# Turning attention weights in 32x32 blocks on VectorE, multiplying with v in eight 32x64 tiles, normalising on ScalarE, and rounding weights by integers

## Chip, cores, metric

One Trainium2 chip, one core. The metric is device time of one execution in microseconds; a kernel's time is the median of its runs. The kernel before: 1921.4 us (1919.91 to 1922.44, 3 runs); with the runs made beside the changed kernel 1921.06 us.

## The reference, cut to what matters

```python
# q, k, v: (8 batches, 8 heads, 576, 64) fp32, tau = 0.02
scores = (q @ k.T) / sqrt(64)
thresh = max(scores, -1) - tau
attn = exp(where(scores >= thresh, scores, -1e9) - max)
attn = attn / (sum(attn) + 1e-9);  o = attn @ v
x = o.transpose(0, 2, 1, 3).reshape(4608, 512)
out = ((x @ w_a) * (x @ w_b)) @ w_out    # w_a, w_b: 512 x 1536, w_out: 1536 x 512, float64 in memory
```

## The kernel before

Attention goes over 32 pairs of heads, five units a pair (four of 128 queries for both heads, one tail of 64 queries each). The feed-forward part of finished blocks (18 blocks of 256 rows) is woven between the units in TensorE's program, so that TensorE has work while the others prepare weights. The weights come as float64 and are turned into fp32 in 36 pieces during the first 18 units. Line numbers in the profiles (L262 and so on) are those of the kernel profiled.

```python
def weigh(i, u):                      # one unit: exp, threshold and sum, normalise
    ...
    nc.scalar.activation(w, s, AF.Exp, bias=..., scale=...)
    nc.vector.scalar_tensor_tensor(out=ws[j], in0=s, scalar=thr, in1=ws[j],
                                   op0=ALU.is_ge, op1=ALU.mult, accum_out=sums)
    nc.vector.reciprocal(rcp[:, 0:n], sums[:, 0:n])
    nc.gpsimd.tensor_scalar(w, w, rcp[:, j:j + 1], None, op0=ALU.mult)      # L262
def turn_pe(i, u):                    # keys to the partitions, by TensorE
    for s in range(4):
        nc.tensor.transpose(tp[:, s, :], w[:, c:c + P], ident)              # L287
    nc.scalar.copy(view[:, 5 * j:5 * j + 4], tp.rearrange(...))             # L288
    ...
def weighted(i, h):                   # half of a pair's queries times v: 128 keys at a time
    nc.tensor.matmul(pv, vd, wT[:, 4, :], start=True, stop=False)           # L355
    for s in range(4):
        for j in range(2):
            nc.tensor.matmul(pv[j*D:(j+1)*D], vm[:, j, s, :], wT[:, 5*j+s, :], ...)  # L358
# main loop, cut
for g in range(len(units) + PV_LAG):
    scores(i, u); turn(*before); weigh(i, u)
    for _ in range(2): convert_weights(); load_weights(1)
    advance(rate)                     # feed-forward matmuls (L388, L404)
    for what in due(g): weighted(*what)
    advance(rate)
```

Of the kernel before, what the change touches and what calls it, by code (L numbers as in the profile page):

```python
# [21 lines left out]
DMA_FROM = 32  # L22
PV_LAG = 1
WT_BUFS = 3
XT_BUFS = 4
W_BUFS = 4
# [3 lines left out]
def kernel(  # L30
# [46 lines left out]
    NSLOT = 9  # L77
    GT = HALF // TAIL
    SCALE = 1.0 / math.sqrt(D)
# [17 lines left out]
    NVD = 3  # L97
    v_diag = [const.tile([P, 2, D], FP32, name=f"v_diag{i}") for i in range(NVD)]

    def load_pair(i):  # L100
# [10 lines left out]
        vm = loads.tile([P, 2, NT, D], FP32, tag="vm", bufs=3, name="vm")  # L111
        vd = v_diag[i % NVD]
        for j in range(2):
            rows = v[b, 2 * hp + j]
            k0 = TAIL * j
            nc.sync.dma_start(vm[:, j], rows[k0:k0 + MAIN].rearrange("(s p) d -> p s d", p=P))
            k0 = MAIN * (1 - j)
            nc.sync.dma_start(vd[TAIL * j:TAIL * (j + 1), j, :], rows[k0:k0 + TAIL])
        tiles["v"] = (vm, vd)
# [23 lines left out]
    def convert_weights():  # L143
# [7 lines left out]

        if not raws:
            return
# [3 lines left out]
        t = work.tile([P, CW], FP32, tag="osb", bufs=4, name="t")  # L157
        low = work.tile([P, CW], FP32, tag="osb", bufs=4, name="low")
        top_u, t_u = top.bitcast(U32), t.bitcast(U32)
        nc.scalar.activation(low, lo, AF.Copy, bias=0.0, scale=2.0 ** -52)  # L160
        nc.vector.tensor_scalar(top_u, hi, 0x7FFFFFFF, None, op0=ALU.bitwise_and)
        nc.gpsimd.tensor_scalar(top, top, float_of(0x47F00000), float_of(0x38000000),  # L162
                                op0=ALU.min, op1=ALU.max)
        nc.vector.tensor_scalar(t_u, top_u, 3, 0x3FFFFFFF,
                                op0=ALU.logical_shift_left, op1=ALU.bitwise_and)
        nc.vector.scalar_tensor_tensor(out=top_u, in0=top_u, scalar=0x40000000, in1=t_u,
                                       op0=ALU.bitwise_and, op1=ALU.bitwise_or)
        nc.vector.tensor_scalar(t_u, top_u, 0x7F800000, None, op0=ALU.bitwise_and)
        nc.gpsimd.tensor_tensor(low, low, t, op=ALU.mult)  # L169
        nc.gpsimd.tensor_tensor(low, low, top, op=ALU.add)  # L170
        nc.vector.scalar_tensor_tensor(out=dst.bitcast(U32), in0=hi, scalar=0x80000000,
                                       in1=low.bitcast(U32),
                                       op0=ALU.bitwise_and, op1=ALU.bitwise_or)


    for t in v_diag:
        nc.gpsimd.memset(t, 0.0)
# [4 lines left out]
    ident = const.tile([P, P], FP32, name="ident")  # L182
    make_identity(nc, ident)
# [20 lines left out]
    prepared, scored, weights, turned, tbufs = {}, {}, {}, {}, {}  # L204
# [16 lines left out]
    def scores(i, u):  # L221
        qT, kT, qd = prepared[i]
        n = 2 if u < NT else 1
        sc = [ps_sc.tile([P, S], FP32, tag="sc", name="sc") for _ in range(n)]
# [19 lines left out]
    def weigh(i, u):  # L244
# [15 lines left out]
        nc.vector.reciprocal(rcp[:, 0:n], sums[:, 0:n])  # L260
        for j, w in enumerate(ws):
            nc.gpsimd.tensor_scalar(w, w, rcp[:, j:j + 1], None, op0=ALU.mult)  # L262
        weights[i, u] = ws

    def turned_tile(i, u):

        h = u // 2
        if (i, h) not in turned:
            if u < NT:
                turned[i, h] = work.tile([P, NSLOT, HALF], FP32, tag="wT", bufs=WT_BUFS, name="wT")  # L270
            else:
                turned[i, h] = work.tile([P, NSLOT, TAIL], FP32, tag="wTt", bufs=2, name="wTt")
        return turned[i, h]

    def turn_pe(i, u):

        ws = weights.pop((i, u))
        wT = turned_tile(i, u)
        if u < NT:
            view = wT.rearrange("p s (i t e) -> p s i t e", i=4, e=Q)[:, :, :, u % 2, :]  # L280
            tp = ps_1.tile([P, 4, P], FP32, tag="ps1", name="tp")
            for j, w in enumerate(ws):
                if j == 1:
                    tp = ps_1.tile([P, 4, P], FP32, tag="ps1", name="tp")
                for s in range(4):
                    c = TAIL * j + s * P
                    nc.tensor.transpose(tp[:, s, :], w[:, c:c + P], ident)  # L287
                nc.scalar.copy(view[:, 5 * j:5 * j + 4], tp.rearrange("p s (i e) -> p s i e", e=Q))  # L288
            tp = ps_1.tile([P, P], FP32, tag="ps1", name="tp")
            for j, w in enumerate(ws):  # L290
                r = slice(TAIL * j, TAIL * (j + 1))
                c = MAIN * (1 - j)
                nc.tensor.matmul(tp[r], w[:, c:c + TAIL], ident, start=True, stop=True)  # L293
            nc.scalar.copy(view[:, 4], tp.rearrange("p (i e) -> p i e", e=Q))  # L294
        else:
            w = ws[0]
            tps = []
            for j in range(2):
                r = slice(TAIL * j, TAIL * (j + 1))
                tp = ps_1.tile([P, 4, TAIL], FP32, tag="ps1", name="tp")  # L300
                for s in range(4):
                    c = TAIL * j + s * P
                    nc.tensor.transpose(tp[:, s, :], w[r, c:c + P], ident[r, r])
                tps.append(tp)
# [5 lines left out]
            for j in range(2):  # L310
                nc.scalar.copy(wT[:, 5 * j:5 * j + 4], tps[j])
                r = slice(TAIL * j, TAIL * (j + 1))
                nc.scalar.copy(wT[r, 4], tp[r, r])

    def turn_dma(i, u):


        ws = weights.pop((i, u))
        wT = turned_tile(i, u)
# [194 lines left out]
```

## Time and profile before

| | busy us | share |
|---|---|---|
| TensorE matmuls (9120) | 1799.5 | 94% |
| GpSimd | 808.2 | 42% |
| VectorE | 711.5 | 37% |
| ScalarE | 559.0 | 29% |

TensorE is dense from 336 us on; before that GpSimd is the busiest and TensorE waits. The prediction below shows the lines. One more line of that page becomes important afterwards, the fetch of TensorE's own instructions in the table of DMA queues (queue, kind: packets, MB, share of 16 engines):

```profile
q8 instruction: 72, 1.18, 0.2%
```

A fetch is 1.18 MB / 72 = 16 KB. TensorE runs 9120 matmuls and as many weight loads, 18240 / 72 = 253 instructions per fetch. Over the dense stretch such a fetch comes about every 24 us. TensorE does not wait for one there: from 336 to 1720 us its waits add up to 0.9 us, for GpSimd.

### The profile page before, as it was taken

The numbers are of one execution on the slowest core, as the hardware profiler recorded it, in microseconds if no ns is written. First come the engines' busy times: TensorE is split into PE (matmuls) and PEld (weight loads), VectorE is DVE, ScalarE is ACT, GpSimd is POOL, SyncE is SP. The second block draws the span as 40 slices with busy tenths as digits, with TensorE's granted clock in tenths as the row PEclk, the third lists the DMA queues (q8 is the fetch of TensorE's own instructions).
The fourth block names the chain that finished last, engine by engine and source line by source line (L and its number), as shares of the span: only waits on it lengthen the run. The fifth ranks groups of instructions, "written<-read, shape, count | busy, mean of one in ns | idle before, by whom it ended". The sixth has DMA issues, their size and how long they took to land.

```text
span 1917.2 us, 24375 instructions
## 1 busy us (share of the span) xinstructions
PE 1799.5 (94%) x9120; PEld 1219.7 (64%) x9120; DVE 711.5 (37%) x1650; ACT 559.0 (29%) x1185; POOL 808.2 (42%) x1047
## 2 busy tenths in 40 slices
PE   4665868999999999999999999999999999999999
PEld 2333545676757575757576767676757575758766
DVE  4666565343334333434333332332334333331000
ACT  2333322333333332333332222222323332331000
POOL 5788777434444344444444323323444344440000
PEclk9666789999999999999999999999999999999999
DMA  4223232111110111111111011001110100000000
GB/s 106 65 64 89 74 96 58 30 19 30 19 30 15 28 20 30 20 30 20 22 21 25 19 25 18 24 13 30 20 30 17 27 13 18 1 12 1 11 11 11
DMA packets 201157, 58.20 MB, mean 30 GB/s; under 512 B 191824, under 2 KB 191824, under 8 KB 201040
## 3 DMA queue, kind: packets, MB, share of 16 engines
q1 hardware_dynamic: 195792, 47.21, 11.6%
q10 hardware_dynamic: 5248, 9.44, 1.4%
q8 instruction: 72, 1.18, 0.2%
q14 instruction: 45, 0.37, 0.1%
HBM read 47.19 MB, written 9.44 MB: 30 GB/s over the span
## 4 chain that ended last, share of the span: by engine, by line
PE 84%; POOL 9%; DVE 4%; issue 2%; ACT 1%; SPq 0%; DMA 0%; POOLq 0%; DVEq 0%; ACTq 0%
PE pab L388 39%; PE po L404 20%; PE sc L229 7%; PE pv L358 6%; PE tp L287 6%; POOL w L262 4%; PE tp L293 2%; POOL low L170 2%; POOL low L169 2%; PE sc L232 2%; PE pv L355 1%; DVE w L255 1%; POOL bias L240 1%; POOL top L162 1%; DVE mx L239 1%
## 5 line engine op out<-in xcount | busy, mean ns | idle before, releaser
L262 POOL TENSOR_SCALAR w<-w,rcp 128x576 f32<-128x576 f32 x288 | 505.9, 1767 | 360.0 <-DVE rcp L260 354.0
L239 DVE TENSOR_REDUCE mx<-sc 128x1 f32<-128x576 f32 x288 | 207.3, 752 | 528.4 <-PE sc L229 458.2
L388 PE MATMUL pab<-xT,wb_sb 128*128 128x256 f32 x1536 | 389.8, 389 | 4.5 <-ACT wT L288 3.2
L404 PE MATMUL po<-wo_sb,h 128*128 128x512 f32 x864 | 389.5, 599 | 0.0
L388 PE MATMUL pab<-xT,wa_sb 128*128 128x256 f32 x1536 | 380.0, 387 | 7.2 <-ACT wT L294 7.2
L388 PEld LDWEIGHTS pab<-xT,wa_sb 128*128 128x128 f32 x1536 | 288.4, 191 | 66.0 <-issue 21.0
L388 PEld LDWEIGHTS pab<-xT,wb_sb 128*128 128x128 f32 x1536 | 287.6, 192 | 55.9 <-issue 10.5
L240 POOL TENSOR_SCALAR bias<-mx,e_nscale 128x1 f32<-128x1 f32 x288 | 95.2, 331 | 472.0 <-DVE mx L239 298.2
L255 DVE SCALAR_TENSOR_TENSOR w<-sc,thr,w 128x576 f32<-128x576 f32 x288 | 226.7, 815 | 142.0 <-ACT w L252 137.9
L404 PEld LDWEIGHTS po<-wo_sb,h 128*128 128x128 f32 x864 | 159.3, 190 | 184.0 <-issue 183.0
L288 ACT COPY wT<-tp 128x512 f32<-128x512 f32 x256 | 138.9, 588 | 415.6 <-PE tp L287 409.0
L252 ACT ACTIVATE w<-sc,bias,e_scale 128x576 f32<-128x576 f32 x288 | 230.3, 846 | 72.8 <-POOL bias L240 72.0
L398 DVE TENSOR_TENSOR h<-a,pab 128x256 f32<-128x256 f32 x216 | 90.6, 420 | 405.7 <-PE pab L388 405.3
L229 PE MATMUL sc<-kT,qT 64*128 64x512 f32 (+1 forms) x1024 | 200.8, 474 | 39.1 <-DVE w L255 30.9
L229 PEld LDWEIGHTS sc<-kT,qT 64*128 64x128 f32 x1024 | 105.9, 198 | 163.6 <-issue 153.3
L287 PE MATMUL tp<-ident,w 128*128 128x128 f32 x1024 | 152.5, 291 | 51.2 <-POOL w L262 51.1
L395 ACT COPY a<-pab 128x256 f32<-128x256 f32 x216 | 80.7, 374 | 364.0 <-PE pab L388 363.9
L287 PEld LDWEIGHTS tp<-ident,w 128*128 128x128 f32 x1024 | 116.9, 148 | 67.1 <-POOL w L262 61.3
L358 PE MATMUL pv<-wT,vm 128*64 128x256 f32 x1024 | 132.7, 404 | 0.0
L358 PEld LDWEIGHTS pv<-wT,vm 128*64 128x64 f32 x1024 | 71.3, 144 | 54.6 <-issue 29.2
L241 POOL TENSOR_SCALAR thr<-mx,cut 128x1 f32<-128x1 f32 x288 | 85.8, 298 | 0.0
L363 ACT COPY xT<-pv 128x256 f32<-128x256 f32 x64 | 23.8, 372 | 199.1 <-PE pv L358 186.6
(55 smaller groups left out, 990.4 us busy)
## 6 DMA issues: line engine op xcount, KB each, us to landing
qm<-in_q_dram SPq DMA_DIRECT2D x128, 72.0 KB, 2.4
km<-in_k_dram SPq DMA_DIRECT2D x128, 72.0 KB, 2.5
vm<-in_v_dram SPq DMA_DIRECT2D x64, 128.0 KB, 2.5
out_dram<-osb ACTq DMA_DIRECT2D x32, 256.0 KB, 2.0
raw<-in_moe_w_a_dram SPq DMA_DIRECT2D x12, 512.0 KB, 3.8
raw<-in_moe_w_b_dram SPq DMA_DIRECT2D x12, 512.0 KB, 3.8
raw<-in_moe_w_out_dram SPq DMA_DIRECT2D x12, 512.0 KB, 3.7
v_diag<-in_v_dram SPq DMA_DIRECT2D x64, 16.0 KB, 2.0
```

What stands on the lines that cost most here:

```text
L229: nc.tensor.matmul(sc[j][:, c0:c1], qT[r, u * P:(u + 1) * P], kT[r, c0:c1], start=True, stop=True)
L239: nc.vector.tensor_reduce(mx[:, c], sc[j], axis=AX.X, op=ALU.max)
L240: nc.gpsimd.tensor_scalar(bias[:, c], mx[:, c], e_nscale[:, 0:1], None, op0=ALU.mult)
L252: nc.scalar.activation(w, s, AF.Exp, bias=bias[:, j:j + 1], scale=e_scale[:, 0:1])
L255: nc.vector.scalar_tensor_tensor(out=ws[j], in0=s, scalar=thr[:, j:j + 1], in1=ws[j], op0=ALU.is_ge, op1=ALU.mult, accum_out=sums[:, j:j + 1])
L262: nc.gpsimd.tensor_scalar(w, w, rcp[:, j:j + 1], None, op0=ALU.mult)
L287: nc.tensor.transpose(tp[:, s, :], w[:, c:c + P], ident)
L288: nc.scalar.copy(view[:, 5 * j:5 * j + 4], tp.rearrange("p s (i e) -> p s i e", e=Q))
L358: nc.tensor.matmul(pv[j * D:(j + 1) * D], vm[:, j, s, :], wT[:, 5 * j + s, :], start=False, stop=(s == 3))
L388: nc.tensor.matmul(p, w[:, c, fs], xT[:, c, :], start=(c == 0), stop=(c == HP - 1))
L398: nc.vector.tensor_tensor(hid, a, pab[1], op=ALU.mult)
L404: nc.tensor.matmul(po, hs[F][:, u * P:(u + 1) * P], wo_sb[:, F, :], start=(F == 0), stop=(F == NF - 1))
```

## The change

The intent: take the transposes off TensorE, the bound engine. VectorE's transpose, as used here (0.77 us for 128x576 in the trace), turns each block of 32x32 in its place, which leaves the keys of each quarter of queries on a partition quadrant of their own; so v is loaded into all four quadrants, and the product is made of eight small tiles (four quadrants of 32 keys, two heads of 64 columns). ScalarE normalises instead of GpSimd, and the conversion of weights needs two buffers a piece instead of three and ends in an integer addition.

```diff
-            nc.gpsimd.tensor_scalar(w, w, rcp[:, j:j + 1], None, op0=ALU.mult)
+            nc.scalar.activation(w, w, AF.Copy, scale=rcp[:, j:j + 1])
...
+        for j in range(2):                       # instead of turn_pe
+            nc.vector.transpose(tb[r, j * NB:(j + 1) * NB, e],
+                                w[r].rearrange("p (n e) -> p n e", e=Q))
...
+        for h in range(2):                       # instead of the five matmuls a half
+            tb = turned.pop((i, h))
+            for c in range(NB):                  # 18 blocks of 32 keys
+                for g in range(G):               # 4 quadrants
+                    for j in range(2):           # 2 heads
+                        n = 3 * Q if h == 1 and g // 2 == j else 2 * Q
+                        nc.tensor.matmul(pv[g][jc, c0:c0 + n], vr[r, j * NB + c, :],
+                                         tb[r, j * NB + c, 0:n],
+                                         start=(c == 0), stop=(c == NB - 1))
...
+        for g in range(G):                       # v, four times
+            nc.sync.dma_start(vr[g * Q:(g + 1) * Q], rows)
...
-        t = work.tile([P, CW], FP32, tag="osb", bufs=4, name="t")
...
-        nc.gpsimd.tensor_tensor(low, low, t, op=ALU.mult)
-        nc.gpsimd.tensor_tensor(low, low, top, op=ALU.add)
-        nc.vector.scalar_tensor_tensor(out=dst.bitcast(U32), in0=hi, scalar=0x80000000,
-                                       in1=low.bitcast(U32),
-                                       op0=ALU.bitwise_and, op1=ALU.bitwise_or)
+        nc.gpsimd.tensor_tensor(dst.bitcast(U32), top_u, low_u, op=ALU.add)
...
-        advance(rate)
-        for what in due(g):
-            weighted(*what)
+        advance(1.7 * rate)
+        if g > NT and g % (NT + 1) == 0:
+            done = g // (NT + 1) - 1
+            weighted(done)
...
-        advance(rate)
+        advance(0.3 * rate)
```

A piece of weights now takes two buffers of the four instead of three, and three instructions on ScalarE, two on VectorE and two on GpSimd instead of one, five and three. The product of a whole pair is one run of matmuls, once every five units.

More of the change, by code (lines that the diff above doesn't have):

```diff
@@ L20, in float_of @@
     return struct.unpack("<f", struct.pack("<I", bits))[0]
-DMA_FROM = 32
-PV_LAG = 1
-WT_BUFS = 3
 XT_BUFS = 4
-W_BUFS = 4
+W_BUFS = 5
+TB0_BUFS = 2
+TB1_BUFS = 1
 @with_exitstack
@@ L76 @@
     HALF = MAIN // 2
-    NSLOT = 9
     GT = HALF // TAIL
+    G = P // Q
+    BANK = 512
     SCALE = 1.0 / math.sqrt(D)
@@ L96 @@
     loaded = {}
-    NVD = 3
-    v_diag = [const.tile([P, 2, D], FP32, name=f"v_diag{i}") for i in range(NVD)]
     def load_pair(i):
@@ L110, in load_pair @@
             tiles[name] = t
-        vm = loads.tile([P, 2, NT, D], FP32, tag="vm", bufs=3, name="vm")
-        vd = v_diag[i % NVD]
-        for j in range(2):
-            rows = v[b, 2 * hp + j]
-            k0 = TAIL * j
-            nc.sync.dma_start(vm[:, j], rows[k0:k0 + MAIN].rearrange("(s p) d -> p s d", p=P))
-            k0 = MAIN * (1 - j)
-            nc.sync.dma_start(vd[TAIL * j:TAIL * (j + 1), j, :], rows[k0:k0 + TAIL])
-        tiles["v"] = (vm, vd)
+        vr = loads.tile([P, 2 * NB, D], FP32, tag="vr", bufs=2, name="vr")
+        rows = v[b, 2 * hp:2 * hp + 2].rearrange("j (n e) d -> e (j n) d", e=Q)
+        for g in range(G):
+            nc.sync.dma_start(vr[g * Q:(g + 1) * Q], rows)
+        tiles["v"] = vr
         loaded[i] = tiles
@@ L156, in convert_weights @@
         top = work.tile([P, CW], FP32, tag="osb", bufs=4, name="top")
-        t = work.tile([P, CW], FP32, tag="osb", bufs=4, name="t")
         low = work.tile([P, CW], FP32, tag="osb", bufs=4, name="low")
-        top_u, t_u = top.bitcast(U32), t.bitcast(U32)
-        nc.scalar.activation(low, lo, AF.Copy, bias=0.0, scale=2.0 ** -52)
-        nc.vector.tensor_scalar(top_u, hi, 0x7FFFFFFF, None, op0=ALU.bitwise_and)
-        nc.gpsimd.tensor_scalar(top, top, float_of(0x47F00000), float_of(0x38000000),
+        top_u, low_u = top.bitcast(U32), low.bitcast(U32)
+        nc.scalar.activation(top, hi.bitcast(FP32), AF.Abs)
+        nc.scalar.activation(low, lo, AF.Copy, bias=2.0 ** 23, scale=2.0 ** -29)
+        nc.gpsimd.tensor_scalar(top, top, float_of(0x47EFFFFF), float_of(0x38000000),
                                 op0=ALU.min, op1=ALU.max)
-        nc.vector.tensor_scalar(t_u, top_u, 3, 0x3FFFFFFF,
+        nc.scalar.activation(low_u, low, AF.Copy, bias=-(2.0 ** 23), scale=1.0)
+        nc.vector.tensor_scalar(top_u, top_u, 3, 0x3FFFFFFF,
                                 op0=ALU.logical_shift_left, op1=ALU.bitwise_and)
-        nc.vector.scalar_tensor_tensor(out=top_u, in0=top_u, scalar=0x40000000, in1=t_u,
+        nc.vector.scalar_tensor_tensor(out=top_u, in0=hi, scalar=0xC0000000, in1=top_u,
                                        op0=ALU.bitwise_and, op1=ALU.bitwise_or)
-        nc.vector.tensor_scalar(t_u, top_u, 0x7F800000, None, op0=ALU.bitwise_and)
-        nc.gpsimd.tensor_tensor(low, low, t, op=ALU.mult)
-        nc.gpsimd.tensor_tensor(low, low, top, op=ALU.add)
-        nc.vector.scalar_tensor_tensor(out=dst.bitcast(U32), in0=hi, scalar=0x80000000,
-                                       in1=low.bitcast(U32),
-                                       op0=ALU.bitwise_and, op1=ALU.bitwise_or)
-    for t in v_diag:
-        nc.gpsimd.memset(t, 0.0)
+        nc.gpsimd.tensor_tensor(dst.bitcast(U32), top_u, low_u, op=ALU.add)
     tau_sb = const.tile([P, 1], FP32, name="tau_sb")
@@ L181 @@
     load_weights(2)
-    ident = const.tile([P, P], FP32, name="ident")
-    make_identity(nc, ident)
     q_diag = [const.tile([P, P], FP32, name=f"q_diag{i}") for i in range(2)]
@@ L201 @@
     nc.vector.tensor_tensor(cut, cut, big, op=ALU.add)
-    prepared, scored, weights, turned, tbufs = {}, {}, {}, {}, {}
+    prepared, scored, weights, turned = {}, {}, {}, {}
     x_of, xtail_of = {}, {}
@@ L223, in scores @@
         n = 2 if u < NT else 1
-        sc = [ps_sc.tile([P, S], FP32, tag="sc", name="sc") for _ in range(n)]
+        sc = [ps_sc.tile([P, 2 * BANK], FP32, tag="sc", name="sc")[:, 0:S] for _ in range(n)]
         for c0, c1 in ((0, MAIN), (MAIN, S)):
@@ L260, in weigh, with turn @@
         nc.vector.reciprocal(rcp[:, 0:n], sums[:, 0:n])
+        weights[i, u] = (ws, rcp)
+    def turn(i, u):
+        ws, rcp = weights.pop((i, u))
         for j, w in enumerate(ws):
-            nc.gpsimd.tensor_scalar(w, w, rcp[:, j:j + 1], None, op0=ALU.mult)
-        weights[i, u] = ws
-    def turned_tile(i, u):
-        h = u // 2
-        if (i, h) not in turned:
-            if u < NT:
-                turned[i, h] = work.tile([P, NSLOT, HALF], FP32, tag="wT", bufs=WT_BUFS, name="wT")
-            else:
-                turned[i, h] = work.tile([P, NSLOT, TAIL], FP32, tag="wTt", bufs=2, name="wTt")
-        return turned[i, h]
@@ L275, in turn_pe @@
-    def turn_pe(i, u):
-        ws = weights.pop((i, u))
-        wT = turned_tile(i, u)
-        if u < NT:
-            view = wT.rearrange("p s (i t e) -> p s i t e", i=4, e=Q)[:, :, :, u % 2, :]
-            tp = ps_1.tile([P, 4, P], FP32, tag="ps1", name="tp")
-            for j, w in enumerate(ws):
-                if j == 1:
-                    tp = ps_1.tile([P, 4, P], FP32, tag="ps1", name="tp")
-                for s in range(4):
-                    c = TAIL * j + s * P
-                    nc.tensor.transpose(tp[:, s, :], w[:, c:c + P], ident)
-                nc.scalar.copy(view[:, 5 * j:5 * j + 4], tp.rearrange("p s (i e) -> p s i e", e=Q))
-            tp = ps_1.tile([P, P], FP32, tag="ps1", name="tp")
-            for j, w in enumerate(ws):
-                r = slice(TAIL * j, TAIL * (j + 1))
-                c = MAIN * (1 - j)
-                nc.tensor.matmul(tp[r], w[:, c:c + TAIL], ident, start=True, stop=True)
-            nc.scalar.copy(view[:, 4], tp.rearrange("p (i e) -> p i e", e=Q))
-        else:
-            w = ws[0]
-            tps = []
-            for j in range(2):
-                r = slice(TAIL * j, TAIL * (j + 1))
-                tp = ps_1.tile([P, 4, TAIL], FP32, tag="ps1", name="tp")
-                for s in range(4):
-                    c = TAIL * j + s * P
-                    nc.tensor.transpose(tp[:, s, :], w[r, c:c + P], ident[r, r])
-                tps.append(tp)
-            tp = ps_1.tile([P, P], FP32, tag="ps1", name="tp")
-            for j in range(2):
-                r = slice(TAIL * j, TAIL * (j + 1))
-                c = MAIN * (1 - j)
-                nc.tensor.matmul(tp[r], w[:, c:c + TAIL], ident, start=True, stop=True)
-            for j in range(2):
-                nc.scalar.copy(wT[:, 5 * j:5 * j + 4], tps[j])
-                r = slice(TAIL * j, TAIL * (j + 1))
-                nc.scalar.copy(wT[r, 4], tp[r, r])
@@ L315, in turn_dma @@
-    def turn_dma(i, u):
-        ws = weights.pop((i, u))
-        wT = turned_tile(i, u)
-        if u < NT:
-            if u % 2 == 0:
-                tbufs[i] = work.tile([P, 2 * NB, 2 * Q], FP32, tag="tb", bufs=2, name="tb")
-            tb = tbufs[i]
-            for j, w in enumerate(ws):
-                nc.vector.transpose(
-                    tb[:, j * NB:(j + 1) * NB, (u % 2) * Q:(u % 2 + 1) * Q],
-                    w.rearrange("p (n e) -> p n e", e=Q))
-            if u % 2 == 0:
-                return
-            src = tb.rearrange("p (s r) e -> p s r e", r=4)
-            for g in range(4):
-                for r in range(4):
-                    nc.sync.dma_start(
-                        wT[r * Q:(r + 1) * Q, :, g * 2 * Q:(g + 1) * 2 * Q],
-                        src[g * Q:(g + 1) * Q, :, r, :])
-        else:
-            tb = work.tile([P, NB, Q], FP32, tag="tbt", bufs=2, name="tbt")
-            nc.vector.transpose(tb.rearrange("p n e -> p (n e)"), ws[0])
-            for g in range(4):
-                j = g // 2
-                for r in range(4):
-                    s = [s for s in range(NSLOT) if 0 <= 4 * s + r - j * NB < NB]
-                    b0 = 4 * s[0] + r - j * NB
-                    nc.sync.dma_start(
-                        wT[r * Q:(r + 1) * Q, s[0]:s[-1] + 1, (g % 2) * Q:(g % 2 + 1) * Q],
-                        tb[g * Q:(g + 1) * Q, b0:b0 + 4 * len(s) - 3:4, :])
@@ L348, in weighted @@
-    def weighted(i, h):
-        b, hp = pairs[i]
-        wT = turned.pop((i, h))
-        vm, vd = loaded[i]["v"]
-        n = HALF if h < 2 else TAIL
-        pv = ps_1.tile([P, n], FP32, tag="ps1", name="pv")
-        nc.tensor.matmul(pv, vd.rearrange("p j d -> p (j d)"), wT[:, 4, :], start=True, stop=False)
-        for s in range(4):
-            for j in range(2):
-                nc.tensor.matmul(pv[j * D:(j + 1) * D], vm[:, j, s, :], wT[:, 5 * j + s, :],
-                                 start=False, stop=(s == 3))
-        if h < 2:
-            if hp == 0:
-                x_of[b, h] = work.tile([P, HP, HALF], FP32, tag="xT", bufs=XT_BUFS, name="xT")
-            nc.scalar.copy(x_of[b, h][:, hp, :].rearrange("p (t i e) -> p i t e", t=2, e=Q),
-                           pv.rearrange("p (i t e) -> p i t e", t=2, e=Q))
-            if hp == HP - 1:
-                blocks.append((x_of.pop((b, h)), ("half", b, h)))
-        else:
-            t = b % GT
-            if hp == 0 and t == 0:
-                xtail_of[b // GT] = work.tile([P, HP, HALF], FP32, tag="xt", bufs=2, name="xt")
-            xt = xtail_of[b // GT]
-            nc.scalar.copy(xt[:, hp, t * TAIL:(t + 1) * TAIL], pv)
-            if hp == HP - 1 and t == GT - 1:
@@ new lines, in turn @@
+            nc.scalar.activation(w, w, AF.Copy, scale=rcp[:, j:j + 1])
+        h = min(u // 2, 1)
+        if u == 0:
+            turned[i, 0] = work.tile([P, 2 * NB, 2 * Q], FP32, tag="tb0", bufs=TB0_BUFS, name="tb0")
+        if u == 2:
+            turned[i, 1] = work.tile([P, 2 * NB, 3 * Q], FP32, tag="tb1", bufs=TB1_BUFS, name="tb1")
+        tb = turned[i, h]
+        e = slice((u - 2 * h) * Q, (u - 2 * h + 1) * Q)
+        for j in range(2):
+            r = slice(0, P) if u < NT else slice(j * D, (j + 1) * D)
+            w = ws[j] if u < NT else ws[0]
+            nc.vector.transpose(tb[r, j * NB:(j + 1) * NB, e],
+                                w[r].rearrange("p (n e) -> p n e", e=Q))
@@ new lines, in weighted @@
+    def weighted(i):
+        b, hp = pairs[i]
+        vr = loaded[i]["v"]
+        pvs = [ps_sc.tile([P, 2 * BANK], FP32, tag="sc", name="pv") for _ in range(2)]
+        pv = [pvs[g // 2][:, (g % 2) * BANK:(g % 2 + 1) * BANK] for g in range(G)]
+        c0 = 0
+        for h in range(2):
[4 more added lines that the diff above has]
+                        n = 3 * Q if h == 1 and g // 2 == j else 2 * Q
+                        r = slice(g * Q, (g + 1) * Q)
+                        jc = slice(j * D, (j + 1) * D)
+                        nc.tensor.matmul(pv[g][jc, c0:c0 + n], vr[r, j * NB + c, :],
+                                         tb[r, j * NB + c, 0:n],
+                                         start=(c == 0), stop=(c == NB - 1))
+            c0 += 2 * Q
+        t = b % GT
+        if hp == 0:
+            for h in range(2):
+                x_of[b, h] = work.tile([P, HP, HALF], FP32, tag="xT", bufs=XT_BUFS, name="xT")
+            if t == 0:
+                xtail_of[b // GT] = work.tile([P, HP, HALF], FP32, tag="xt", bufs=2, name="xt")
+        xt = xtail_of[b // GT][:, hp, t * TAIL:(t + 1) * TAIL]
+        for gg in range(2):
+            for h in range(2):
+                x = x_of[b, h][:, hp, :].rearrange("p (t g e) -> p t g e", t=2, g=G)
+                nc.scalar.copy(
+                    x[:, :, 2 * gg:2 * gg + 2, :],
+                    pvs[gg].rearrange("p (g c) -> p g c", g=2)[:, :, 2 * Q * h:2 * Q * (h + 1)]
+                    .rearrange("p g (t e) -> p t g e", t=2))
+            jc = slice(gg * D, (gg + 1) * D)
+            nc.scalar.copy(xt[jc].rearrange("p (g e) -> p g e", g=2),
+                           pvs[gg][jc].rearrange("p (g c) -> p g c", g=2)[:, :, 4 * Q:5 * Q])
+        if hp == HP - 1:
+            for h in range(2):
+                blocks.append((x_of.pop((b, h)), ("half", b, h)))
+            if t == GT - 1:
@@ L374, in weighted @@
                 blocks.append((xtail_of.pop(b // GT), ("tail", b - t, 0)))
-            del loaded[i], prepared[i]
+        del loaded[i], prepared[i]
     def ffn(xT, what):
@@ L442 @@
     UB = HP * (NT + 1)
-    def turn(i, u):
-        (turn_dma if i >= DMA_FROM else turn_pe)(i, u)
-    def due(g):
-        got = []
-        for d, first, last in ((PV_LAG, 1, 1), (PV_LAG, 3, 3), (PV_LAG, 4, 4)):
-            if g - d >= 0 and units[g - d][1] == last:
-                got.append((units[g - d][0], last // 2))
-        return got
     prep(0)
@@ L457 @@
     rate = 0.0
-    for g in range(len(units) + PV_LAG):
+    for g in range(len(units) + 2):
         if g < len(units):
             i, u = units[g]
-            if u == 0 and i + 1 < NPR:
+            if u == 1 and i + 1 < NPR:
                 load_pair(i + 1)
@@ L474 @@
             before = (i, u)
-        advance(rate)
-        for what in due(g):
-            weighted(*what)
-            if what[1] == 1 and what[0] % HP == HP - 1:
+        advance(1.7 * rate)
+        if g > NT and g % (NT + 1) == 0:
+            done = g // (NT + 1) - 1
+            weighted(done)
+            if pairs[done][1] == HP - 1:
                 rate = backlog() / (2 * UB)
-        advance(rate)
+        advance(0.3 * rate)
     advance(float("inf"))
```

## The prediction

> **What bounds the kernel now.** I read the page first: busy shares, the slices of the span, the chain of waits by engine.
>
> ```profile
> PE 1799.5 (94%) x9120; PEld 1219.7 (64%) x9120; DVE 711.5 (37%) x1650; ACT 559.0 (29%) x1185; POOL 808.2 (42%) x1047
> ...
> PE   4665868999999999999999999999999999999999
> ...
> POOL 5788777434444344444444323323444344440000
> PEclk9666789999999999999999999999999999999999
> ...
> PE 84%; POOL 9%; DVE 4%; issue 2%; ACT 1%; SPq 0%; DMA 0%; POOLq 0%; DVEq 0%; ACTq 0%
> ```
>
> There are two stages. In the first seven slices (to 336 us) TensorE is at 4 to 8 tenths, GpSimd at 7 to 8, and the granted clock is low. From 336 us to the end TensorE never stops; there only TensorE work counts. So I need TensorE's work per pair of heads and the idle time of the first stage. The work I take from the timeline of TensorE in the dense stretch, as the distance from one group's start to the next (the ends are modelled):
>
> ```profile
> 1009.57 0.59 PE L355 MATMUL pv<-wT,v_diag 128*128 128x256 f32 x2
> 1010.09 1.95 PE L358 MATMUL pv<-wT,vm 128*64 128x256 f32 x16
> 1011.97 1.99 PE L388 MATMUL pab<-xT,wa_sb 128*128 128x256 f32 x8
> ...
> 1020.21 0.33 PE L355 MATMUL pv<-wTt,v_diag 128*128 128x64 f32 x2
> 1020.47 0.69 PE L358 MATMUL pv<-wTt,vm 128*64 128x64 f32 x16
> 1021.08 1.13 PE L388 MATMUL pab<-xT,wb_sb 128*128 128x256 f32 x4
> ...
> 1024.30 1.30 PE L229 MATMUL sc<-kT,qT 64*128 64x512 f32 x8
> 1025.53 1.09 PE L287 MATMUL tp<-ident,w 128*128 128x128 f32 x8
> 1026.55 0.44 PE L293 MATMUL tp<-ident,w 128*64 128x128 f32 x4
> 1026.92 1.56 PE L388 MATMUL pab<-xT,wb_sb 128*128 128x256 f32 x6
> ```
>
> The scores of a unit take 1025.53 - 1024.30 = 1.23 us, its transposes 1.39 us; half a product with v takes 2.40 us, its tail 0.87 us. A pair has four such units and a tail unit (in the same timeline scores about 1.0, transposes 0.76). Per pair: scores 5.9, transposes 4 x 1.39 + 0.76 = 6.3, product 2 x 2.40 + 0.87 = 5.7 us. One block of the feed-forward part, undisturbed at the end, takes 41.4 + 20.6 = 62.0 us (192 and 48 matmuls in the chain of waits), 18 blocks 1117 us. In the dense stretch its matmuls take 32 us more than that rate, at the handovers. Sum: 32 x 17.9 + 1117 + 32 = 1722 us, so about 195 us of 1917 is TensorE idle or slow, nearly all in the first stage.
>
> The first stage, by stretches of the span (columns: stretch, length, busy us of PE, PEld, DVE, ACT, POOL, clock, DMA share, GB/s) and groups of instructions:
>
> ```profile
> 20.00:240.00 220.00, 146.70 (x661) 85.08 (x662) 132.83 (x276) 73.21 (x139) 173.72 (x191) 0.71 0.29 72
> ...
> L262 POOL TENSOR_SCALAR w<-w,rcp 128x576 f32<-128x576 f32 x288 | 505.9, 1767 | 360.0 <-DVE rcp L260 354.0
> ...
> L170 POOL TENSOR_TENSOR low<-low,top 128x512 f32<-128x512 f32 x36 | 47.7, 1326 | 2.3
> L169 POOL TENSOR_TENSOR low<-low,t 128x512 f32<-128x512 f32 x36 | 45.6, 1267 | 32.2 <-DVE t L168 16.3 <-DVE sums L258 8.9 <-DVE rcp L260 5.9
> ...
> L213 DVE STREAM_TRANSPOSE qT<-qm 128x576 f32<-128x576 f32 x32 | 24.6, 768 | 1.5 <-DMA qm<-in_q_dram 1.5
> ```
>
> GpSimd is busy 79% of this stretch: per unit 1.8 normalisations of 1.77 us, plus two weight pieces of 0.63 + 1.27 + 1.33 us, plus 1.1 us of small work: 10.8 us. The reciprocals show 20 units done at 218 us, 10.9 us each, and the 36th piece of weights at 328 us, 9 us apiece: a piece takes three of four buffers, so pieces go one at a time.
>
> [...] in the tail product two matmuls start 6 to 7 ns apart in every 58 ns, and each mode change leaves about 0.15 us. [...] No stretch of this trace shows a sustained rate above about 70 instructions a microsecond. [...] the trace has 72 fetches of 16 KB.
>
> **The change, part by part.**
> - *Transposes off TensorE*: -6.3 us per pair, -202 us. VectorE gets ten block transposes of 0.77 us per pair, 7.7 us (+246 us), beside TensorE: its load of 37% rises to near 50%.
> - *The product with v*: 18 key blocks x 8 tiles x 2 parts of queries = 288 fp32 products a pair, each two passes: 576 matmuls and 576 weight loads, against about 66 matmuls now. Call its time X. A pass of 64 columns lasts 58 ns (tail product); 96 columns scale to about 85. With all eight tiles at once X = 18 x 2 x (58 + 85) ns + two drains = 5.5 us. That needs a pass every 7 ns or so, weight load included, kept up over 1152 instructions. I doubt that and allow 7 ns for each instruction, weight load or matmul: X = 8.1 us.
> - *Normalising to ScalarE*: GpSimd loses 506 us; ScalarE gains 288 x about 0.7 us (from its 0.59 us for 512 columns) = 200 and loses the copies of transposes (139 + 36 + 21 + 13 = 209 us). Both are hidden when dense.
> - *Integer rounding*: a piece costs GpSimd 0.63 + 1.3, VectorE two instructions of 0.43 and 0.73 instead of five of 3.1 in all, ScalarE three of about 0.67. With two buffers of four, two pieces can be on their way.
> - *v to four quadrants*: 4608 packets of 256 bytes a pair instead of 1152, about 5 us of all DMA engines at 18.5 ns each; hidden when dense, felt in the first stage.
>
> First stage after: per unit GpSimd 5.0 us, ScalarE 1.8 x (0.85 + 0.7) + 4.0 + 0.4 = 7.2, VectorE 1.4 + 1.5 + 1.6 + 2.3 + 0.7 = 7.5. With waits between them 8.5 us: the 20 units until the feed-forward part can start take 170 us, of which TensorE works 4 x (5.9 + about 7) = 50. Idle: 120 us instead of 195. DMA needs about 135 us there (18.9 MB of weights at 200 GB/s plus 41 of q, k, v), under 170.
>
> Dense work: 1117 + 32 x 5.9 = 1306, plus 24 for fewer handovers. The product takes both score buffers of PSUM, and only 0.3 of a share of feed-forward work (about 1 us) covers its six copies out (1.5 to 2 us on ScalarE): about 0.8 us stall a pair, 25 us. End 5 us. Span = 1306 + 24 + 120 + 25 + 5 + 32 X = 1480 + 32 X. With X = 8.1: 1739 us; I say 1740.
>
> **Rivals.**
> 1. *Full packing*, X = 5.5: 1656 us. For it: two row tiles (scores) and two column tiles already overlap fully. Against it: no trace line has more than two tiles.
> 2. [...]
> 3. *Only two tiles overlap*[...]: X = 288 x 58 ns + 1.9 = 18.6, 2075 us. Against it: in the trace two passes of *different* tiles start together[...].
> 4. *Fetch of instructions*: 74 KB per burst, a 16 KB fetch takes about 1 us in the trace. If buffers hold little, X is about 9 to 15.
> 5. *Another engine becomes the bound*: VectorE near 50% and ScalarE near 35% speak against it outside the first stage.
>
> **Range and chances.** The first stage is worth 75 us in nearly any case; the rest hangs on X, with break-even at (1917 - 1480) / 32 = 13.7 us. I give full packing to 8 us 40%, 8 to 12.4 us 26%, 12.4 to 15 us (within 2% of even, or just under) 8%, above that 26%. Range 1645 to 2000; faster 0.66, same 0.08, slower 0.26.
>
> **What would show it.** TensorE's timeline should have one burst of 576 matmuls per pair: its length is X[...]. The reciprocal of the 20th unit should come near 170 us, the last weight piece before it. GpSimd should fall near 260 us busy, VectorE rise near 880. A gap after the burst, ended by ScalarE's copies, should be under 1 us. I am wrong if the burst takes over 13.7 us, if the engine waits in it for instructions, or if the first stage stays near 300 us because another chain (weights, DMA) takes GpSimd's place.

Some figures above have no line beside them; these are of the same trace. One fp32 product of the program is two matmuls in it (L355: one call a half, x2). The scores' matmuls (64 rows, 512 columns) start in twos, 7 ns apart, every 430 ns, where the feed-forward ones of 512 columns start singly every 429 ns. The 0.15 us of a mode change is the distance from the last start of the tail product (1020.93) to the next group (1021.08), and the two drains in X are two of these. The 36864 packets of 256 bytes took 18.5 ns in the mean. The 200 GB/s is an estimate from the first 20 us, 165 GB/s at a DMA share of 0.81. The 7 ns allowed for each instruction is an estimate; what was measured beside it are the starts 6 to 7 ns apart.

## The result

| | before | changed |
|---|---|---|
| time, median us (range) | 1921.06 (1919.91 to 1922.44) | 1980.62 (1978.76 to 1984.01) |
| VectorE / ScalarE / GpSimd busy us | 711.5 / 559.0 / 808.2 | 878.5 / 621.7 / 246.6 |
| TensorE matmul instructions | 9120 | 23904 |
| reciprocal of the 20th unit, us | 217.6 | 209.9 |
| last piece of weights, us | 327.9 | 245.8 |

The ratio is 1.031 (95% interval 1.029 to 1.033): slower. Ratios in this document are the mean time of one kernel's fast runs over that of the other's of the same rounds, so not quite the ratio of the medians quoted.

The page of the changed kernel: busy shares, slices, DMA queue of TensorE's instructions, the chain of waits by engine, the product's group.

```profile
PE 1717.4 (87%) x23904; PEld 1239.8 (63%) x23904; DVE 878.5 (44%) x1862; ACT 621.7 (31%) x1129; POOL 246.6 (12%) x718
...
PE   2565598889998998899989999889998998989999
...
PEclk9765598999989888899999998889989998999999
...
q8 instruction: 188, 3.08, 0.7%
...
PE 85%; issue 9%; DVE 3%; POOL 2%; ACT 1%; DMA 0%; SPq 0%; DVEq 0%; POOLq 0%
...
L282 PE MATMUL pv<-tb,vr 32*64 32x64 f32 (+1 forms) x18432 | 314.5, 282 | 170.5 <-issue 170.4
```

Before, TensorE was at nine tenths in every slice from the eighth on. Now eights and nines alternate, and the granted clock dips with them. The new thing in the chain is "issue", up from 2% to 9%: time in which the engine waited for nothing that the profile shows. TensorE's waits of this kind all stand before one line, the product with v: 170 us. The timeline of one product in the dense stretch shows where:

```profile
998.16 0.59 PE L321 MATMUL pab<-xT,wa_sb 128*128 128x256 f32 x2
998.69 3.22 PE L282 MATMUL pv<-tb,vr 32*64 32x64 f32 x274
1003.79 1.78 PE L282 MATMUL pv<-tb,vr 32*64 32x64 f32 x128 [1.88 <-issue]
1007.53 1.82 PE L282 MATMUL pv<-tb,vr 32*64 32x64 f32 x128 [1.97 <-issue]
1011.55 0.85 PE L282 MATMUL pv<-tb,vr 32*64 32x64 f32 x46 [2.20 <-issue]
1012.34 2.63 PE L321 MATMUL pab<-xT,wa_sb 128*128 128x256 f32 x6
1014.90 1.87 PE L215 MATMUL sc<-kT,qT 64*128 64x512 f32 x8
```

The 576 matmuls run in stretches with a stop of about 2 us between them, and the stretches inside are of exactly 128. With a weight load each, 128 matmuls are 256 instructions: one fetch (3.08 MB / 188 = 16 KB here too, and 47808 / 188 = 254 instructions). In all 32 products the first stop (over 0.5 us) comes after 86 to 274 matmuls, and the later ones 128 apart, but for one of the first stage.

The DMA records of the trace, counted from the start of the span like the lines above, have fetches that start at 997.92, 1001.37, 1004.90 and 1009.12 us, 3.5 to 4.2 us apart instead of 24. The last three take 0.9 to 1.3 us, and TensorE goes on 1.3 to 1.5 us after each has landed. It is so at all 111 stops of the 32 products: each ends 0.4 to 1.6 us (median 1.4) after a fetch has landed.

From 998.69 to 1012.34 the product takes 13.65 us; the mean over the 32 products is 14.9 us, of which 5.9 us are stops. Stops are counted here, and in all runs below, as distances of over 0.5 us from one matmul's start to the next, 190 us in all; the profile's idle time is a little less, 157 us inside the products and 14 us before them.

Two smaller things are in the same lines. Inside a stretch the eight tiles do run together: the first 32 matmuls of this burst start 6 to 7 ns apart in rounds of eight, the second and third round 58 to 59 ns long (the first is 106), as long as two tiles took for one pass each of 64 columns in the tail product before (58 ns). From the 33rd on the pace slackens to 11 to 12 ns a matmul in the first half of the columns. And after the burst six feed-forward matmuls take 2.56 us up to the next group where six take 1.3 elsewhere, and a score group takes 1.79 us instead of 1.23: the granted clock was halved (0.5 in the clock records). In this case the record runs from 1012.7 to 1016.1 us, where the feed-forward matmuls start 427 ns apart instead of 216. After 400 us there are 222 us of such time, against 2 us in the kernel before, which lie behind its last matmul; here each halved stretch but the one at the very end (4 us) begins inside a product or at most 0.4 us after it.

The first stage, as a stretch of the span, answers to the line the prediction shows of before:

```profile
20.00:240.00 220.00, 117.43 (x2476) 84.65 (x2477) 134.67 (x262) 116.86 (x198) 89.70 (x146) 0.67 0.54 116
```

GpSimd fell from 173.72 to 89.70 us, ScalarE rose from 73.21 to 116.86, and TensorE is busy even less than before. The times of the reciprocals show why: most units follow each other within 12 us, but after the first unit of a pair, where the product of the pair before stands in the program, there are 34, 25, 24 and 27 us. With no feed-forward work beside it the first four bursts lasted 17.0, 17.3, 15.8 and 15.9 us (after the first, TensorE waited 6.1 us more for a copy on ScalarE); the clock was halved for 9, 61, 100 and 78% of them.

### The profile page after: what moved, and what is told of

Its sections match the earlier page's. It is cut to its first block, busy times and chain, and to the rows that moved or that the text cites. A ratio compares the mean times of both kernels' runs of the same rounds, so it can differ in the third digit from the quotient of the medians.

```text
span 1976.9 us, 53536 instructions
## 1 busy us (share of the span) xinstructions
PE 1717.4 (87%) x23904; PEld 1239.8 (63%) x23904; DVE 878.5 (44%) x1862; ACT 621.7 (31%) x1129; POOL 246.6 (12%) x718
## 3 DMA queue, kind: packets, MB, share of 16 engines
q8 instruction: 188, 3.08, 0.7%
## 4 chain that ended last, share of the span: by engine, by line
PE 85%; issue 9%; DVE 3%; POOL 2%; ACT 1%; DMA 0%; SPq 0%; DVEq 0%; POOLq 0%
PE pab L321 39%; PE po L337 19%; PE pv L282 15%; PE sc L215 9%; PE sc L218 2%; DVE w L241 1%; DVE top L161 1%; DVE mx L225 1%; POOL top L156 0%; POOL wa_sb L163 0%; DVE tb L264 0%; DVE top L159 0%; POOL bias L226 0%; ACT w L253 0%; ACT w L238 0%
## 5 line engine op out<-in xcount | busy, mean ns | idle before, releaser
L282 PE MATMUL pv<-tb,vr 32*64 32x64 f32 (+1 forms) x18432 | 314.5, 282 | 170.5 <-issue 170.4
L282 PEld LDWEIGHTS pv<-tb,vr 32*64 32x64 f32 x18432 | 282.5, 163 | 208.3 <-issue 201.4
L321 PE MATMUL pab<-xT,wa_sb 128*128 128x256 f32 x1536 | 399.9, 397 | 6.1 <-ACT xT L296 6.1
L321 PE MATMUL pab<-xT,wb_sb 128*128 128x256 f32 x1536 | 374.4, 383 | 0.0
L264 DVE STREAM_TRANSPOSE tb<-w 128x576 f32<-128x576 f32 (+1 forms) x320 | 239.3, 767 | 123.8 <-ACT w L253 123.1
L253 ACT ACTIVATE w<-w,rcp 128x576 f32<-128x576 f32 x288 | 212.7, 771 | 194.0 <-DVE rcp L246 194.0
L215 PEld LDWEIGHTS sc<-kT,qT 64*128 64x128 f32 x1024 | 115.6, 211 | 199.8 <-issue 174.4
L296 ACT COPY xT<-pv 128x128 f32<-128x128 f32 x128 | 27.7, 272 | 430.0 <-PE pv L282 429.2
L341 ACT COPY osb<-po 128x512 f32<-128x512 f32 x36 | 20.8, 579 | 116.1 <-PE po L337 116.1
L218 PE MATMUL sc<-kT,q_diag 128*128 128x64 f32 (+1 forms) x128 | 42.8, 461 | 10.4 <-DVE w L241 10.4
```

Source lines behind the costliest of these rows:

```text
L215: nc.tensor.matmul(sc[j][:, c0:c1], qT[r, u * P:(u + 1) * P], kT[r, c0:c1], start=True, stop=True)
L253: nc.scalar.activation(w, w, AF.Copy, scale=rcp[:, j:j + 1])
L264: nc.vector.transpose(tb[r, j * NB:(j + 1) * NB, e], w[r].rearrange("p (n e) -> p n e", e=Q))
L282: nc.tensor.matmul(pv[g][jc, c0:c0 + n], vr[r, j * NB + c, :], tb[r, j * NB + c, 0:n], start=(c == 0), stop=(c == NB - 1))
L321: nc.tensor.matmul(p, w[:, c, fs], xT[:, c, :], start=(c == 0), stop=(c == HP - 1))
```

## The experiments

The theory after reading: TensorE runs out of instructions. The first stop came after 172 to 548 of them (86 to 274 matmuls), 256 more came with each fetch, 3.5 to 4.2 us apart in the burst shown, and the product asks for 1152 in a row. Rivals: the stops belong to the tiles (PSUM, data, array); or the cost lies in another part of the change.

| run | what | us (median) | ratio to before | 95% interval |
|---|---|---|---|---|
| changed kernel | | 1980.62 | 1.031 | 1.029 to 1.033 |
| e1_four_tiles | four tiles overlap instead of eight | 2113.23 | 1.100 | 1.099 to 1.102 |
| e2_pieces | the product in four pieces | 1851.77 | 0.965 | 0.962 to 0.967 |
| e3_one_tb | half the instructions | 1725.78 | 0.899 | 0.897 to 0.900 |
| e4_rounding_only | before + conversion | 1867.34 | 0.972 | 0.971 to 0.974 |
| e5_norm_only | before + ScalarE normalises | 1878.48 | 0.978 | 0.976 to 0.979 |
| e6_one_tb_two_pieces | e3, product in two pieces | 1702.05 | 0.886 | 0.885 to 0.888 |
| e7_one_tb_four_tiles | e3 with four tiles | 1849.53 | 0.963 | 0.962 to 0.965 |
| e8_one_tb_early_qk | e6, q and k earlier | 1701.23 | 0.886 | 0.884 to 0.887 |
| e9_rounding_and_norm | before + both | 1846.10 | 0.962 | 0.960 to 0.964 |
| e10_convert_last | e6, conversion later | 1704.53 | 0.887 | 0.886 to 0.889 |

All ten results were correct against the reference.

**e3_one_tb: the same columns in half the instructions**

```diff
-turned[i, 0]: [P, 2 * NB, 2 * Q] (2 buffers);  turned[i, 1]: [P, 2 * NB, 3 * Q] (1 buffer)
+turned[i] = work.tile([P, 2 * NB, 5 * Q], FP32, tag="tb", bufs=1, name="tb")
-        for h in range(2):
-            for c in range(NB):  ... n = 64, or 64 and 96
+        for c in range(NB):      ... n = 160, or 128
```

> The changed kernel with one buffer for all turned weights of a pair, so that one matmul takes 160 or 128 columns instead of two of 64 and 64 or 96: half the instructions for the same columns. Fetch theory: 576 instructions a burst instead of 1152[...]; 36 passes of 0.138 us = 5.0 us, drains, and at most one or two gaps: burst 6 to 8 us, time 1700 to 1760 us. Rival (columns streamed, or the array, set the burst): burst stays near 14 us, time 1960 to 1990 us.

Measured 1725.78 us, as expected; the rival is out. One product of it:

```profile
871.82 3.33 PE L276 MATMUL pv<-tb,vr 32*64 32x160 f32 x177
876.05 2.16 PE L276 MATMUL pv<-tb,vr 32*64 32x160 f32 x111 [0.90 <-issue]
878.13 1.56 PE L314 MATMUL pab<-xT,wa_sb 128*128 128x256 f32 x6
```

There is one stop where there were three or four, of 0.90 us where those were of about 2, and the burst lasts 6.3 us. Over all products the median is 6.4 us and the stops are 1.0 us a product (5.9 in the changed kernel). The halved clock after 400 us fell from 222 us to 4 us, all of it at the very end (mean granted clock 0.961 against 0.901). The columns streamed are the same.

**e2_pieces: the same instructions, spread**

```diff
+                if (h * NB + c + 1) % 9 == 0 and h * NB + c + 1 < 2 * NB:
+                    between()        # lambda: advance(0.67 * rate)
-        advance(1.7 * rate) before each product, advance(0.3 * rate) after
+        1.2 before, 0.67 in each of three pauses, 0.3 after; 1.625 in the other units
```

> The changed kernel, the same matmuls of the product cut into four pieces with about 2 us of feed-forward matmuls between them (as much feed-forward work as before over a pair). Fetch theory: nearly all the 170 us in which the product waits for issue go; against it four more changes of tiling mode a pair at about 0.2 us each (25 us in all); time 1830 to 1870 us. Rival (the waits belong to PSUM, the array or the data of the product, not to the fetch): the waits stay, time 1980 to 2010 us.

Measured 1851.77 us, as expected. Two of the four pieces of one product, and what lies around them:

```profile
934.10 1.80 PE L282 MATMUL pv<-tb,vr 32*64 32x64 f32 x144
...
939.05 1.80 PE L282 MATMUL pv<-tb,vr 32*64 32x64 f32 x144
940.78 1.13 PE L324 MATMUL pab<-xT,wa_sb 128*128 128x256 f32 x4
```

A piece of 144 matmuls runs through in 1.73 us (940.78 - 939.05), 12 ns each, with no stop inside. The waits for issue went from 170 to 78 us, not to "nearly all": 41 us of them lie after 300 us (134 in the changed kernel). The rest is in the first stage, where there is no feed-forward work to put between the pieces. The same matmuls stall or don't according to how densely they stand in the program: together with the fetches that land 0.4 to 1.6 us before each restart in the changed kernel, that is the supply of instructions, not the tiles. The halved clock after 400 us fell to 43 us (mean granted clock 0.949).

**e1_four_tiles: half the overlap**

```diff
-            for c in range(NB):
-                for g in range(G):
+            for g0 in (0, 2):
+              for c in range(NB):
+                for g in (g0, g0 + 1):
```

> The changed kernel, but the product runs over two quadrants of v first and then over the other two, so four tiles can overlap instead of eight; same instructions, same columns. Theory (the burst is paced by the fetch of instructions, 256 at a time every 3.5 us): the stretches of 128 matmuls get longer and the gaps between them shorter, the burst stays 14.5 to 15.5 us, time 1975 to 2010 us. Rival (the burst is paced by how many tiles overlap): stretches of 128 matmuls double from about 1.8 and 2.8 us, gaps stay near 2 us, burst about 21 us, time about 2180 us.

Measured 2113.23 us: a miss for both. The burst took 17.8 us in the mean (15.5 expected at most), though its stops shrank from 5.9 to 2.2 us as the theory said.

```profile
1068.43 4.11 PE L283 MATMUL pv<-tb,vr 32*64 32x64 f32 x273
1074.18 3.04 PE L283 MATMUL pv<-tb,vr 32*64 32x64 f32 x128 [1.64 <-issue]
1077.93 6.75 PE L283 MATMUL pv<-tb,vr 32*64 32x96 f32 x175 [0.70 <-issue]
1084.61 2.93 PE L322 MATMUL pab<-xT,wa_sb 128*128 128x256 f32 x6
```

The first 273 matmuls run at 15 ns, what four tiles give at the full clock (58 / 4). The last 175 take 38 ns each instead of the 21 that I estimate for 96 columns (85 / 4, with the prediction's 85), and the feed-forward matmuls after them are twice as long as usual. The clock was halved in the middle of the burst; the mean granted clock was 0.866 against 0.901, and the halved time after 400 us 420 us against 222. So a burst with half the tiles and stops costs clock as well. I had not reckoned with the clock, and this run can't separate the two.

**e7_one_tb_four_tiles: the overlap again, without the stops**

```diff
-        for c in range(NB):
-            for g in range(G):
+        for c, g in [(c, g0 + d) for g0 in (0, 2) for c in range(NB) for d in range(2)]:
```

> e3_one_tb, but two quadrants of v first, then the other two: four tiles overlap instead of eight, same instructions. With the fetch out of the way the overlap should count: 72 passes of 0.138 us = 9.9 us instead of 5.0, less the gap: burst 9.9 to 10.5 us instead of 6.4 (7.4 in the mean, with the first pairs), time 1835 to 1880 us, provided the granted clock stays at full. If the overlap of eight isn't real: no change from 1726 us.

Measured 1849.53 us, as expected: 124 us over e3.

```profile
953.52 9.54 PE L275 MATMUL pv<-tb,vr 32*64 32x160 f32 x288
962.99 1.56 PE L313 MATMUL pab<-xT,wa_sb 128*128 128x256 f32 x6
```

The burst has no stop: 288 matmuls with their weight loads in 9.47 us are 16.4 ns an instruction, and the changed kernel was supplied with 256 every 3.5 us or so, 14 ns each. A pass takes 9.47 / 72 = 0.132 us (0.138 was the estimate), and after 400 us the clock is full but for 4 us at the very end (0.956 in the mean of the run, first stage included). Eight tiles against four are worth 9.47 - 6.4 = 3.1 us a product, and 4.2 us against the 5.3 us of the next run, which has no stop either. The packing of eight tiles works; it was hidden behind the fetch in the changed kernel (5.9 us of stops a product).

**e6_one_tb_two_pieces: half the instructions and spread**

```diff
+            if (c + 1) % 9 == 0 and c + 1 < NB:
+                between()            # lambda: advance(0.5 * rate)
-        1.7 and 0.3 around the product; 2.0 in the other units
+        1.7, 0.5 and 0.4;              1.85 in the other units
```

> e3_one_tb with the product cut once in the middle, about 1.5 us of feed-forward matmuls in between. Fetch theory: the one gap of about 1 us a pair (32 us in all) goes, two mode changes of 0.1 to 0.2 us come: time 1695 to 1720 us against 1726. Rival (the gap isn't the fetch): the gap stays, 1726 to 1740 us.

Measured 1702.05 us, as expected: both pieces go in 2.66 us each without a stop, 5.3 us in all. (Before the dense stretch 12 us of waits for issue remain.)

```profile
860.56 2.73 PE L276 MATMUL pv<-tb,vr 32*64 32x160 f32 x144
863.22 0.70 PE L316 MATMUL pab<-xT,wa_sb 128*128 128x256 f32 x2
...
866.00 2.73 PE L276 MATMUL pv<-tb,vr 32*64 32x160 f32 x144
868.66 1.56 PE L316 MATMUL pab<-xT,wa_sb 128*128 128x256 f32 x6
```

**e4_rounding_only, e5_norm_only and e9_rounding_and_norm: the other parts on the kernel before**

e4 takes the two-buffer conversion with integer rounding into the kernel before, e5 this one line, e9 both:

```diff
-            nc.gpsimd.tensor_scalar(w, w, rcp[:, j:j + 1], None, op0=ALU.mult)
+            nc.scalar.activation(w, w, AF.Copy, scale=rcp[:, j:j + 1])
```

> The kernel before with only the new conversion of the weights (two buffers a piece, integer rounding). Theory of the prediction: in the first stage the pieces of weights no longer go one at a time, the last piece comes before 230 us instead of 328 us, dense work starts earlier; time 1860 to 1890 us. Rival (GpSimd's normalisations keep the first stage where it is): 1910 to 1925 us.

> The kernel before with only the normalisation moved from GpSimd to ScalarE. Theory (in the first stage the pieces of weights go one at a time and set its end; GpSimd's normalisations only share its time): the last piece comes a little sooner, before 328 but after 280 us, time 1890 to 1920 us. Rival (GpSimd's load of 79% sets the first stage): the last piece before 240 us, time about 1860 us.

> The kernel before with the new conversion of the weights and the normalisation on ScalarE, that is, the change without its third part (turning by VectorE, eight tiles, v in four quadrants). Alone they gave 53 and 42 us. Theory (both shorten the first stage only, and share what they shorten): 1825 to 1855 us, so the third part costs 125 to 155 us. Rival (the changed kernel's first stage gained all that is to be had, or one part hides the other): 1860 us or more.

Rounding alone: 1867.34 us, the last piece of weights at 214 us instead of 328, as expected. Normalisation alone: 1878.48 us, a larger gain than the theory's 1890 to 1920 us, with the last piece at 284 us. I take it that the pieces still go one at a time and GpSimd is freer between them; no run tests that. Both: 1846.10 us, the last piece at 187 us, the 20th unit at 190 us. The same stretch as above, of e9:

```profile
20.00:240.00 220.00, 176.69 (x846) 107.86 (x846) 128.06 (x264) 155.56 (x287) 98.10 (x166) 0.75 0.40 105
```

GpSimd is at 45% (79% before) and TensorE gained 30 us in this stretch. So these two parts give 75 us, and the third part (turning, tiles, v four times) costs 1980.6 - 1846.1 = 134.5 us on top of them.

**e8_one_tb_early_qk and e10_convert_last: the first stage of e6**

```diff
 e8
-            if u == 1 and i + 1 < NPR: load_pair(i + 1)
+            if u == 0 and i + 1 < NPR: load_pair(i + 1)     # q, k
+            if u == 1 and i + 1 < NPR: load_v(i + 1)
 e10
-            convert_weights(); load_weights(1)  (twice)  before the product
+            the same at the end of the unit, after it
```

> e6 with q and k of the next pair asked for one unit earlier than v (as early as the kernel before did). Theory (three waits for q and k in the first stage, 32 us in e3, come from the later loads and from v's four-fold loads ahead in the queue): the waits go, time 20 to 35 us under e6. Rival (they are only replaced by other waits of the first stage): within 10 us of e6.

> e6 with the conversion of weights asked for at the end of a unit, behind the product and its copies, instead of before them. Theory (after the first pair TensorE waits 20.7 us because ScalarE, which now has three conversion steps a piece, does conversions ahead of the copy of the product that the next matmul needs): that wait goes, time 1670 to 1695 us against 1702. Rival (the conversions are needed anyway and another wait takes its place): 1695 to 1710 us.

In both the theory missed and the rival came true: 1701.23 and 1704.53 us, within 3 us of e6. In e8 the waits for k fell from 31.8 to 16.2 us, and those for the product's copies on ScalarE rose from 22.7 to 36.2 us. In e10 the longest wait for the first copy,

```profile
PE pab L316 <- ACT xT L291: 20.7, 1, 20.7
```

(this is e6: TensorE's waits, columns total, times, longest) fell to 15.3 us only, and other waits grew. The first stage has several chains of nearly the same length; what sets its end with the small product stays open.

## Why the prediction was wrong

The direction was wrong: 1740 us and a gain of 9% foretold, 1980.6 us and a loss of 3% measured, though inside the wide range. The sum "1480 + 32 X" was nearly right: with the measured X of 14.9 us it gives 1957 us of span, and the span was 1976.9. That is partly luck: the 25 us allowed for copies measured 7, which hides part of what the first stage and the clock cost more. Two of the prediction's own signs of being wrong came true: the burst took over 13.7 us, and the engine waited in it for instructions.

- **The step that failed** is "I doubt that and allow 7 ns for each instruction, weight load or matmul: X = 8.1 us." The matmuls outside the stops did take that: 14.9 - 5.9 = 9.0 us with the stretches at a halved clock in it. What the term left out are the stops, 5.9 us a product, 190 us in all. Rival 4 named the fetch, with an estimated range that holds the result ("X is about 9 to 15"), but it stood fourth of five, and no chance was given to it by name. The evidence for the choice was in part in the trace of before: a fetch each 253 instructions, taking 0.9 to 1.9 us, so 1152 instructions in 5 to 8 us needed four or five fetches, one every 1 to 2 us. What that trace could not show is how closely fetches can follow each other: after 400 us they were never less than 18 us apart there, and in the changed kernel never less than 3.3. That TensorE would have the instructions of a burst at hand was assumed, not shown. The cause is shown by e2, which changes the spacing of the instructions alone, by e3, which halves their number for the same columns (and uses one buffer), and by the fetches that land 0.4 to 1.6 us before each restart of the changed kernel.
- **Rivals 1 and 3.** Full packing is real (e7 against e3: eight tiles are worth 3.1 us a product) but not reached over 1152 instructions: matmuls start 6 to 7 ns apart in the first 32, 12 ns apart after that and in the pieces of e2. Only two tiles overlapping is refuted by the same starts, eight in a round of 58 to 59 ns. The mean over a whole product, 14.9 us / 576 = 26 ns, is no pace of its own: it is the mean of stretches at 12 ns or somewhat more and of stops.
- **The first stage.** "The first stage is worth 75 us in nearly any case": on the kernel before, the two parts that concern it gave just 75 us (e9). In the changed kernel they arrived in part only: the 20th unit came at 210 us, not 170. There the step that failed is "TensorE works 4 x (5.9 + about 7) = 50", since the first four bursts took 66 us instead of 28. With the product small (e3) the 20th unit still came at 211 us, so further waits lie behind; e8 and e10 did not remove them.
- **Not foreseen: the clock.** The prediction had no term for it. Outside the product, from 320 us on, scores cost 161.3 us for 928 matmuls against 156.5 for 964 in the kernel before, and the first feed-forward layer 226.1 ns a matmul against 223.1: from these two rates I estimate 20 us in all. It went where the stops went (e3 and e7: 4 us halved), but not in proportion to them: e1 has fewer stops and 420 us. What sets it off stays open.
- **Right.** Transposes off TensorE: product plus transposes cost 12.1 us a pair before (326 us for the 27 pairs after 320 us) and 5.3 in e6. VectorE 878 us busy (880 foretold), GpSimd 247 (260). A stall by the copies out of PSUM after the burst was allowed 25 us; TensorE's waits for them (total, times, longest) add up to 7.0 us, nearly all of it after the first product:

```profile
PE pab L321 <- ACT xT L296: 6.1, 1, 6.1
PE sc L215 <- ACT xt L301: 0.9, 3, 0.4
```

- **A wrong count without weight.** The prediction has "about 66 matmuls now" for the product of a pair in the kernel before. It is 54: 18 in each half, 18 in the tail (lines L355 and L358). No sum rests on it.

The balance against the kernel before: 32 x (14.9 - 12.1) = 90 us more for product and transposes, some 20 us for the clock. A difference of 60 us was measured, so the first stage kept about 50 us of its 75; that last figure is what is left over, not a measurement.

## What to carry to other kernels

Before cutting a matmul into small tiles, count instructions per microsecond, not only columns: here TensorE was supplied with 256 instructions every 3.5 us (the median from one restart to the next after 400 us; 27 ns for a matmul with its weight load) once the first 172 to 548 were used up, and 1152 in a row lost 6 us where the columns needed about 5. Make each instruction longer first (160 columns instead of 64 took 1981 to 1726 us), then spread the burst among long matmuls (1702 us). The sign in a profile is a wait for "issue" between stretches of the same round number of instructions (here waits of about 2 us, 170 us in the run, and stretches of 128 matmuls), with a fetch of instructions landing just before each restart (0.4 to 1.6 us). When records of different kinds are paired, count all of them from the same start of the span: the raw times of this trace begin 11.0 us before it.
